# An attention and expert-routing kernel whose instruction order is searched anew

## The chip, the cores and the metric

The kernel runs on one core of a Trainium2 chip. The metric is the device time of one execution in microseconds (us). The kernel before takes 164.45 us, the median of three runs (163.86 to 164.68). One execution more was recorded by the hardware profiler, and everything that is read from a trace comes from that one.

The core's engines run their own instruction lists side by side. PE multiplies matrices into PSUM, DVE and ACT work on vectors, POOL does small work, and SP issues DMAs. An engine takes its instructions strictly in the order of its list and stands still until what the next one needs is there.

## The reference

The input x holds 4 batches of 11,456 rows of 128 numbers; there are 32 inducing rows, and 8 experts of two layers each. Two attentions follow each other, and the result goes through a layer of experts, of which each row takes the best one:

```python
def mab(q, kv):
    s = scale * (q @ kv.transpose(0, 2, 1))
    s = s - s.max(-1, keepdims=True)
    a = np.exp(s)
    a /= a.sum(-1, keepdims=True) + 1e-09
    return a @ kv
h = mab(I, x)
return mab(x, h).astype(np.float32)
...
logits = x @ w_gate
expert_idx = np.argmax(logits, axis=1)
...
    h = np.maximum(xe @ w1[e], 0.0)
    ye = h @ w2[e]
    out[mask] = gate_w[mask, None] * ye
```

The first attention sums over all rows of a batch, so the second can begin only when the batch's 32 rows of h are complete. What the experts see is a mixture of 32 rows, so the kernel applies the batch's expert to these 32 rows once and mixes the results.

## The kernel before

Each batch is cut into 6 groups; group g of batch b has the number k = 6b + g, from 0 to 23. A group is one load of xT (960 KB, tile `big`), and 19 such tiles hold loaded xT, a second form xn of it, and output on its way out. Ten groups load xn as well. For the 14 others PE turns the loaded xT (15 blocks of 128x128) and ACT or DVE copy the result out of PSUM.

For a group the first attention takes a score product (`scores`, 4 matmuls in the list, which the trace records as 8), the maximum, the exponential on ACT, a transpose on DVE, and an H sum (`h_sum`, 15 matmuls in the list, 30 in the trace). After the sixth group a short sequence on DVE, POOL and PE makes the batch's h, its centred form `hc`, the expert's result `h4`, and fetches the expert's weights (1024 KB, `fetch`, issued by ACT into the only `wt` tile).

The second attention reads the same xT tile again: a score product with `hc`, the exponential, and, four groups at a time, a logits product, then gate weights on DVE, a spread product (`spread`), a multiplication on DVE, four expert products (`experts`), four copies to an output tile by ACT or DVE (`evict`), and a store (960 KB). The tile of xT is free once the score product with `hc` has read it. The tile of xn is free once its H sum has read it.

What runs when is set by a program ahead of the chip. `make_plan` writes all operations with what they depend on, `schedule` sorts them into one list per engine, and the kernel is that list. `schedule` plays the execution through with assumed durations and picks, for each engine that is free, the ready operation with the lowest rank. The ranks come from the table `PLAN`. `schedule` also gives out the tiles, so what a load has to wait for follows from the order. In the played execution SP holds back a load or a store while `INFLIGHT` of them are under way:

```python
            if busy[e] > t or (e == "SP" and inflight >= INFLIGHT):
                continue
```

The finished kernel has no such rule. SP waits only for the semaphores that say that the tile is free.

Of the kernel before, what the change touches and what calls it, by code (L numbers as in the profile page):

```python
# [18 lines left out]
B, N, C, M, E, F = 4, 11456, 128, 32, 8, 1024  # L19
P = 128  # L20
# [14 lines left out]
HOP, SAME, FREE, RATE, PAUSE, AGAIN, FIRST = 70, 35, 40, 420, 400, 1200, 490000  # L35
SWITCH, STICK, INFLIGHT, BEHIND = 145, 10990, 2, 27149
# [23 lines left out]
class Lines:  # L60
# [3 lines left out]
    def put(self, o, when):  # L64
        queue, size, weight, start, _ = o.dma
        q, when = self.queues.setdefault(queue, []), when + start
        if queue == "SP" and not q and when - self.last > PAUSE:
            when += AGAIN
        q.append([when, size, weight, o, queue == "SP"])
# [41 lines left out]
def schedule(ops, caps, groups):  # L111
# [54 lines left out]
    while done < len(ops):  # L166
# [75 lines left out]
BYTES = 983040  # L242
LAG = 1060

PLAN = {
    "A": [
        17166, 30860, 22659, 17269, 6624, 4373, 4782, 13983, 33870, 18093, 7605, -6153, 10338, 6743, 1815, -6765,
        12145, 1215, 9171, -11099, 2829, -22378, 9660, 7139,
    ],
    "L": [  # L250
        -22577, -20358, -30968, -27201, -21639, -28610, -16795, -17141, 1480, -31968, -33025, 11502, -3904, 4335,
        11351, 18051, 6540, 8404, 16971, 4643, 15711, 27260, 33194, 28410,
    ],
    "N": [
        7261, 4545, -2957, -33356, 1585, 22336, 20181, -13380, -8654, 15944, 12613, -23335, -3583, -3966, -18329,
        -12841, 6354, 12743, 12327, -31853, 14534, 13707, 30755, 17389,
    ],
    "S": [
        -18320, 7796, 9352, -1925, -14397, -7386, -4476, 18662, 2319, 11122, 3399, -23370, -43944, -18219, -21050,
        -10585, 11208, -34837, 40042, 5734, 21165, 11776, 34515, -3269,  # L260
    ],
    "R": [
        -44906, 56, -24232, -58472, -48981, -57542, -36224, -33903,
    ],
    "X": [
        -31666, 10454, -45613, -16798, -24345, -17218, -24300, 252, -42184, -7384, -58546, -46281, -23642, -37678,
        -7849, -31311, -64290, -24020, -13825, 3252, -15541, -22251, 1326, 1966,
    ],
    "C": [
        4873, -17403, -60296, -10236,  # L270
    ],
    "off": {
# [7 lines left out]
    },  # L280
    "own": {
# [155 lines left out]
def make_plan(K, plan):  # L437
# [28 lines left out]
    for b in range(B):  # L466
        acc = nb_prev = None
        s1, m1, e1 = {}, {}, {}
        xn = {}
        for g in range(NG):  # L470
            k = b * NG + g
# [890 lines left out]
```

## Time and profile before

| quantity | value |
|---|---|
| median of three runs | 164.45 us (163.86 to 164.68) |
| the profiled execution | 164.66 us |
| its span, first to last instruction | 162.9 us |
| PE busy | 144.8 us, 89% |
| DVE busy | 123.0 us, 75% |
| ACT busy | 96.3 us, 59% |
| moved by DMA | 61.88 MB, mean 380 GB/s |

The span is what the trace shows; 1.76 us of the profiled execution's time lie around it. A busy share is a mean over stages with different limits, so the rows below are by stretch. [...] "To landing" is the time from the issue of a DMA to the moment at which its data has arrived; a DMA that waits behind others in the queue has that wait in it.

### The profile page before, as it was taken

How to read it: one execution, taken by the hardware profiler on the slowest of the kernel's cores; microseconds unless marked ns; L12 is line 12 of the kernel's file. 1: busy time of each engine (PE TensorE's matmuls, PEld its weight loads, DVE VectorE, ACT ScalarE, POOL GpSimd, SP SyncE). 2: the span in 40 equal slices, each digit the busy share in tenths (PEclk: the TensorE clock that was granted, in tenths of full speed). 3: DMA queues.
4: the chain of work that ended last, by engine and by line, in shares of the span. 5: the costliest groups of instructions: out<-in, count | busy, mean ns of one | idle time of the engine just before them, and what ended most of it. 6: DMA issues, size and time to landing. Idle time of an engine off the chain costs nothing.

```text
span 162.9 us, 5024 instructions
## 1 busy us (share of the span) xinstructions
PE 144.8 (89%) x1994; PEld 86.7 (53%) x1995; DVE 123.0 (75%) x350; ACT 96.3 (59%) x200; POOL 14.9 (9%) x78
## 2 busy tenths in 40 slices
PE   7799999999989869999999999999999999997000
PEld 4096847789823635385756674565633455363000
DVE  0048569777569986999999999989999999896000
ACT  3043683564247358452687678698989888957000
POOL 0100000000000300021100001331050201120000
PEclk9999999999999999999999999999999999999555
DMA  5999999999999999999998998989999999999991
GB/s 162 428 428 428 419 428 430 417 405 344 365 399 336 426 416 429 394 424 427 423 383 295 260 396 334 415 303 364 423 373 292 427 426 424 424 424 422 416 410 51
DMA packets 9102, 61.88 MB, mean 380 GB/s; under 512 B 1008, under 2 KB 1136, under 8 KB 8560
## 3 DMA queue, kind: packets, MB, share of 16 engines
q1 hardware_dynamic: 8352, 57.10, 87.4%
q10 hardware_dynamic: 720, 4.39, 7.3%
q8 instruction: 17, 0.28, 0.7%
q14 instruction: 13, 0.11, 0.2%
HBM read 37.89 MB, written 23.59 MB: 377 GB/s over the span
## 4 chain that ended last, share of the span: by engine, by line
PE 76%; DMA 12%; DVE 2%; ACT 1%; issue 1%; SPq 0%; DVEq 0%
PE bank L717 21%; PE bank L1019 17%; PE bank L728 14%; PE bank L770 10%; DMA big<-in_xT 9%; PE bank L1012 5%; DMA csb<-in_consts 3%; PE bank L681 3%; PE bank L956 3%; ACT big L736 1%; PE bank L879 1%; PE bank L857 1%; DVE mx L720 0%; DVE mid L961 0%; DVE mid L760 0%
## 5 line engine op out<-in xcount | busy, mean ns | idle before, releaser
L736 ACT COPY big<-bank 128x480 f32<-128x480 f32 (+2 forms) x124 | 61.4, 588 | 31.3 <-PE bank L728 23.2
L1019 PE MATMUL bank<-mid,h 32*128 32x480 f32 x192 | 34.1, 602 | 0.4 <-ACT big L736 0.4
L728 PEld LDWEIGHTS bank<-csb,big 128*128 128x128 f32 x210 | 23.8, 145 | 7.0 <-issue 3.5
L728 PE MATMUL bank<-csb,big 128*128 128x128 f32 x210 | 26.1, 282 | 1.3 <-DVE rs L983 1.3
L717 PE MATMUL bank<-big,csb 128*32 128x480 f32 x192 | 24.5, 589 | 2.3 <-DMA big<-in_xT 1.2
L720 DVE TENSOR_REDUCE mx<-bank 128x1 f32<-128x480 f32 x24 | 15.4, 648 | 11.2 <-PE bank L717 10.4
L770 PE MATMUL bank<-big,mid 128*32 128x129 f32 x720 | 23.8, 274 | 0.0
L770 PEld LDWEIGHTS bank<-big,mid 128*32 128x32 f32 x720 | 21.2, 110 | 4.3 <-issue 3.0
L952 ACT ACTIVATE mid<-bank,nb 128x480 f32<-128x480 f32 x24 | 15.4, 663 | 13.1 <-DVE nb L947 11.2
L1019 PEld LDWEIGHTS bank<-mid,h 32*128 32x128 f32 x192 | 17.0, 183 | 10.3 <-ACT big L736 3.7
L738 DVE COPY big<-bank 128x512 f32<-128x512 f32 (+2 forms) x28 | 17.5, 650 | 5.9 <-PE bank L728 5.2
L717 PE MATMUL bank<-big,hc 128*32 128x480 f32 x192 | 21.4, 568 | 0.0
L757 ACT ACTIVATE mid<-bank,mx 128x480 f32<-128x480 f32 x24 | 14.9, 664 | 3.6 <-DVE mx L754 3.6
L760 DVE STREAM_TRANSPOSE mid<-mid 128x480 f32<-128x480 f32 x24 | 15.2, 652 | 0.7 <-ACT mid L757 0.7
L943 DVE TENSOR_REDUCE mx<-bank 128x1 f32<-128x480 f32 x24 | 14.9, 631 | 1.0 <-PE bank L717 0.9
L1012 PE MATMUL bank<-mid,sel 32*128 32x480 f32 x48 | 15.1, 603 | 0.0
L1015 DVE TENSOR_TENSOR mid<-mid,bank 128x480 f32<-128x480 f32 x24 | 14.8, 644 | 0.2
L717 PEld LDWEIGHTS bank<-big,csb 128*32 128x32 f32 x192 | 5.5, 111 | 9.4 <-issue 3.6
L717 PEld LDWEIGHTS bank<-big,hc 128*32 128x32 f32 x192 | 5.4, 111 | 9.2 <-issue 5.1
L1012 PEld LDWEIGHTS bank<-mid,sel 32*128 32x128 f32 x48 | 5.3, 183 | 3.0 <-ACT big L736 1.4
L956 PE MATMUL bank<-mid,gzb 128*32 128x480 f32 x48 | 6.2, 572 | 0.0
L939 POOL COPY thr_all<-thr 32x1 f32<-32x1 f32 x24 | 4.3, 180 | 9.8 <-DVE thr L932 8.9
(96 smaller groups left out, 117.3 us busy)
## 6 DMA issues: line engine op xcount, KB each, us to landing
big<-in_xT SPq DMA_DIRECT2D x24, 960.0 KB, 10.4
out<-big SPq DMA_DIRECT2D x24, 960.0 KB, 6.8
big<-in_xn SPq DMA_DIRECT2D x10, 967.5 KB, 8.7
wt<-in_w ACTq DMA_DIRECT2D x4, 1024.0 KB, 10.4
csb<-in_consts ACTq DMA_DIRECT2D x1, 194.5 KB, 5.5
```

The source lines that it names most:

```text
L717: self.nc.tensor.matmul(self.blk(ps[32 * q : 32 * q + 32, :GW]), lhsT=lhsT, rhs=x[:, :, q, :], start=True, stop=True)
L720: self.nc.vector.tensor_reduce(self.mx1[b][g // 2][:, g % 2 : g % 2 + 1], self.bank(fe)[:, :GW], AX.X, ALU.max)
L728: self.nc.tensor.transpose(ps[:, k * P : (k + 1) * P], x[:, k0 + k].rearrange("p q t -> p (q t)"), self.ident)
L736: self.nc.scalar.copy(dst, src)
L738: self.nc.vector.tensor_copy(dst, src)
L757: self.nc.scalar.activation(self.at(e), self.bank(fe)[:, :GW], AF.Exp, bias=self.mx1[b][p + 1][:, 2:3], scale=SCALE)
L760: self.nc.vector.transpose(self.at(e), self.at(e))
L770: self.nc.tensor.matmul(ps[32 * j : 32 * j + 32, : P + 1], lhsT=e[:, k, :], rhs=x[:, k, :], start=(n < 4), stop=(n >= 2 * GB - 4))
L943: self.nc.vector.tensor_reduce(self.mx2[r][:, u : u + 1], self.bank(fe)[:, :GW], AX.X, ALU.max)
L952: self.nc.scalar.activation(self.at(e), self.bank(fe)[:, :GW], AF.Exp, bias=self.nb2[r][:, u : u + 1])
L1012: self.nc.tensor.matmul(self.bank(s)[:, :GW], lhsT=self.sel[rows], rhs=self.at(lv)[rows], start=True, stop=True)
L1019: self.nc.tensor.matmul(self.bank(o)[:, :GW], lhsT=self.h4[b][rows], rhs=self.at(e)[rows], start=True, stop=True)
```

## The change

The operations and their number are the same. The search that found the table `PLAN` was run again with another picture of the queue in `schedule`: SP may have three DMAs under way instead of two, so two may be queued behind the one in progress, and a load's data is assumed to start 3000 ns after its issue instead of 1000 (`LEAD`), except at the start of the kernel. Two other constants of the sorting changed, and nearly every number of `PLAN`, of which the diff shows the ranks of the xT loads. `PLAN` also says which engine makes some of the copies out of PSUM: DVE now makes 32 of the copies to `big` tiles instead of 28, ACT 120 instead of 124.

```diff
@@ -33,7 +33,7 @@
 
 
 HOP, SAME, FREE, RATE, PAUSE, AGAIN, FIRST = 70, 35, 40, 420, 400, 1200, 490000
-SWITCH, STICK, INFLIGHT, BEHIND = 145, 10990, 2, 27149
+SWITCH, STICK, INFLIGHT, BEHIND = 145, 10693, 3, 17877
 COLD, IDLE, WINDOW = 6500, 3000, 3400
 ENGINES = ("PE", "DVE", "ACT", "POOL", "SP")
 
@@ -63,8 +63,9 @@
 
     def put(self, o, when):
         queue, size, weight, start, _ = o.dma
+        start = min(start, 1000) if when < 1500 else start
         q, when = self.queues.setdefault(queue, []), when + start
-        if queue == "SP" and not q and when - self.last > PAUSE:
+        if queue == "SP" and not q and when - self.last > PAUSE and start < 2000:
             when += AGAIN
         q.append([when, size, weight, o, queue == "SP"])
 
@@ -241,186 +242,187 @@
 GROUPS = {"mid": (18, {"e1": 6, "e2": 13, "lv": 4}), "bank": (8, {"fe": 6, "o": 8, "mi": 3, "sp": 3}), "big": (19, {"xt": 17, "xn": 6, "ob": 6})}
 BYTES = 983040
 LAG = 1060
+LEAD = 3000
 
 PLAN = {
...
     "L": [
-        -22577, -20358, -30968, -27201, -21639, -28610, -16795, -17141, 1480, -31968, -33025, 11502, -3904, 4335,
-        11351, 18051, 6540, 8404, 16971, 4643, 15711, 27260, 33194, 28410,
+        -33798, -16984, -29552, -24749, -21692, -32969, -33305, -29006, -15841, -4369, 7132, -20776, 12552, 5655,
+        11228, 16108, 6631, 5749, 16403, 5868, 14901, 28644, 33347, 29138,
     ],
...
@@ -472,7 +474,7 @@
             xt = xts[k] = Buf("xt")
             xn[g] = Buf("xn")
             fe = Buf("fe")
-            ld = op(f"LT{k}", ("L", k, ""), {"SP": (400, 400)}, lambda xt=xt, b=b, g=g: K.load_xt(xt, b, g), take=[xt], dma=("SP", BYTES, 7680, 1000, LAG))
+            ld = op(f"LT{k}", ("L", k, ""), {"SP": (400, 400)}, lambda xt=xt, b=b, g=g: K.load_xt(xt, b, g), take=[xt], dma=("SP", BYTES, 7680, LEAD, LAG))
             s1[g] = op(f"S1.{k}", ("A", k, "S1"), pe(800), lambda fe=fe, xt=xt: K.scores(fe, K.it_s, xt), [ld, warm], take=[fe], use=[xt], kind="C")
             m1[g] = op(f"M1.{k}", ("A", k, "M1"), {"DVE": dve(480)}, lambda fe=fe, b=b, g=g: K.max1(fe, b, g), [s1[g]], use=[fe])
             if g in TURNED[b]:
@@ -484,7 +486,7 @@
                     tr = op(f"TR{k}.{n}", ("A", k, "TR"), pe(110 * m), lambda o=o, xt=xt, k0=k0, m=m: K.turn(o, xt, k0, m), [ld, on], take=[o], use=[xt], kind="F")
                     xr.append(op(f"TE{k}.{n}", ("A", k, "TE"), {"ACT": act(m * 128), "DVE": dve(m * 128)}, lambda e, o=o, xn=xn[g], k0=k0, m=m: K.turn_out(e, o, xn, k0, m), [tr, on], use=[o, xn[g]]))
             else:
-                xr = [op(f"LN{k}", ("N", k, ""), {"SP": (400, 400)}, lambda xn=xn[g], b=b, g=g: K.load_xn(xn, b, g), take=[xn[g]], dma=("SP", 990720, 7740, 1000, LAG))]
+                xr = [op(f"LN{k}", ("N", k, ""), {"SP": (400, 400)}, lambda xn=xn[g], b=b, g=g: K.load_xn(xn, b, g), take=[xn[g]], dma=("SP", 990720, 7740, LEAD, LAG))]
             e1[g] = (fe, Buf("e1"), xr)
             if g % 2:
                 p = g // 2

```

In the lists a tile has its buffer number behind its name, so the same number stands again when the buffer is used again. The line numbers of the new kernel are two higher.

The first place is SP, the loads that follow the first eleven. `in_xT` and `in_xn` are the two forms of a group. In the list of before this was:

```order
L708 DMA big_103<-in_xn 128x1935
L705 DMA big_94<-in_xT 128x1920
L708 DMA big_88<-in_xn 128x1935
L708 DMA big_90<-in_xn 128x1935
L705 DMA big_103<-in_xT 128x1920
L705 DMA big_92<-in_xT 128x1920
L708 DMA big_88<-in_xn 128x1935
L708 DMA big_90<-in_xn 128x1935
L705 DMA big_101<-in_xT 128x1920
```

The fifth of these, into `big_92`, is batch 1, group 5. In the new list the loads from the twelfth on read:

```order
L707 DMA big_103<-in_xT 128x1920
L710 DMA big_91<-in_xn 128x1935
L710 DMA big_89<-in_xn 128x1935
L707 DMA big_99<-in_xT 128x1920
L710 DMA big_97<-in_xn 128x1935
L707 DMA big_102<-in_xT 128x1920
L707 DMA big_91<-in_xT 128x1920
L710 DMA big_93<-in_xn 128x1935
L710 DMA big_97<-in_xn 128x1935
L707 DMA big_90<-in_xT 128x1920
```

Batch 1, group 5 is now the first of the rows (`big_103`), ahead of every load that waits for a tile; the xn load into `big_91` and another into `big_89` follow it. The last row, `big_90`, is batch 2, group 3.

The second place is PE, at the first score product of batch 3, group 0 (in `big_97` before, in `big_98` now) and the transposes of batch 2, group 4 (L728 before, L730 now; in `big_93` before, in `big_94` now). Before, it read:

```order
L717 MATMUL bank_83<-big_101,csb 32x480 x4
L681 MATMUL bank_79<-mq_0_151,csb 32x8 x4
L681 MATMUL bank_78<-csb,hacc_170 32x32 x4
L681 MATMUL bank_78<-csb,hacc_170 32x128 x4
L717 MATMUL bank_82<-big_97,csb 32x480 x4
L956 MATMUL bank_81<-mid_117,gzb_195 32x480
L956 MATMUL bank_81<-mid_121,gzb_195 32x480
L956 MATMUL bank_81<-mid_120,gzb_195 32x480
L956 MATMUL bank_81<-mid_115,gzb_195 32x480
L728 MATMUL bank_84<-csb,big_97 128x128 x4
L728 MATMUL bank_77<-csb,big_97 128x128 x4
L728 MATMUL bank_78<-csb,big_93 128x128 x4
```

Now it reads:

```order
L958 MATMUL bank_77<-mid_104,gzb_195 32x480
L719 MATMUL bank_82<-big_98,csb 32x480 x4
L719 MATMUL bank_78<-big_90,csb 32x480 x4
L859 MATMUL bank_81<-wt_128,hT_all 32x256 x4
L730 MATMUL bank_79<-csb,big_98 128x128 x4
L730 MATMUL bank_77<-csb,big_90 128x128 x3
L730 MATMUL bank_84<-csb,big_93 128x128 x3
L730 MATMUL bank_83<-csb,big_93 128x128 x4
L730 MATMUL bank_81<-csb,big_93 128x128 x4
L730 MATMUL bank_79<-csb,big_90 128x128 x4
L730 MATMUL bank_77<-csb,big_94 128x128 x4
```

The score product of batch 3, group 0 now stands behind the four logits matmuls (L956 before, L958 now, of which the last is shown) instead of ahead of them, and eight other products and transposes stand between it and the first transpose of `big_94`, the last row.

The third place is SP again, where the loads end and the stores begin. Before:

```order
L708 DMA big_98<-in_xn 128x1935
L708 DMA big_100<-in_xn 128x1935
L708 DMA big_92<-in_xn 128x1935
L708 DMA big_99<-in_xn 128x1935
L711 DMA out<-big_90 128x1920
L711 DMA out<-big_102 128x1920
```

Now:

```order
L710 DMA big_103<-in_xn 128x1935
L710 DMA big_100<-in_xn 128x1935
L713 DMA out<-big_97 128x1920
L710 DMA big_96<-in_xn 128x1935
L710 DMA big_95<-in_xn 128x1935
L713 DMA out<-big_85 128x1920
L713 DMA out<-big_97 128x1920
```

The first store, batch 0, group 3 from `big_97`, now stands ahead of the last two xn loads (batch 3, groups 3 and 4, into `big_96` and `big_95`).

## Rows read from the trace of the kernel before

**Rows 1.** The page, its span and the DMA rate in 40 slices of 4.07 us.

```profile
span 162.9 us, 5024 instructions
...
GB/s 162 428 428 428 419 428 430 417 405 344 365 399 336 426 416 429 394 424 427 423 383 295 260 396 334 415 303 364 423 373 292 427 426 424 424 424 422 416 410 51
```

**Rows 2.** Windows: stretch, us, busy us of each engine (instructions), PEclk, DMA share, GB/s.

```profile
35.00:63.00 28.00, 25.43 (x449) 16.99 (x443) 21.40 (x64) 14.14 (x29) 1.50 (x8) 1.00 0.98 386
63.00:110.00 47.00, 47.00 (x820) 28.18 (x812) 44.87 (x135) 32.59 (x71) 5.76 (x24) 1.00 0.95 371
110.00:150.00 40.00, 39.45 (x342) 19.14 (x337) 37.61 (x105) 33.68 (x74) 6.45 (x29) 1.00 1.00 401
150.00:159.00 9.00, 0.00 (x0) 0.00 (x0) 0.31 (x1) 0.46 (x1) 0.00 (x0) 0.51 0.99 408
```

**Rows 3.** Windows of two short stretches among the stores.

```profile
109.20:110.40 1.20, 1.20 (x13) 1.01 (x11) 1.17 (x4) 1.20 (x4) 0.08 (x1) 1.00 0.29 116
121.00:126.00 5.00, 5.00 (x61) 1.63 (x53) 4.97 (x16) 4.10 (x9) 0.40 (x1) 1.00 1.00 288
```

**Rows 4.** Timeline of SP: start, length, queue, line, operation, tiles, count.

```profile
49.58 0.48 SPq L705 DMA_DIRECT2D big<-in_xT  x1
...
109.61 0.33 SPq L711 DMA_DIRECT2D out<-big  x1
...
150.91 1.22 SPq L711 DMA_DIRECT2D out<-big  x1
```

**Rows 5.** Single DMA issues at 31.1, 49.6, 85.5, 87.4, 109.6, 119.4, 150.9; all weights.

```profile
big<-in_xn SPq DMA_DIRECT2D x1, 967.5 KB, 6.5
...
big<-in_xT SPq DMA_DIRECT2D x1, 960.0 KB, 11.0
...
big<-in_xn SPq DMA_DIRECT2D x1, 967.5 KB, 5.2
...
big<-in_xn SPq DMA_DIRECT2D x1, 967.5 KB, 7.6
...
out<-big SPq DMA_DIRECT2D x1, 960.0 KB, 5.2
...
out<-big SPq DMA_DIRECT2D x1, 960.0 KB, 11.1
...
out<-big SPq DMA_DIRECT2D x1, 960.0 KB, 10.5
...
wt<-in_w ACTq DMA_DIRECT2D x4, 1024.0 KB, 10.4
```

**Rows 6.** Chain of waits from 36 to 62 us: start, length, what.

```profile
39.66 7.19 DMA big<-in_xT
...
48.77 7.58 DMA big<-in_xT
```

**Rows 7.** Timeline of PE from 44 to 62 us, in brackets its idle time before.

```profile
46.90 1.01 PE L717 MATMUL bank<-big,csb 128*32 128x480 f32 x8 [0.62 <-DMA big<-in_xT]
...
56.49 1.01 PE L717 MATMUL bank<-big,csb 128*32 128x480 f32 x8 [0.62 <-DMA big<-in_xT]
...
60.67 1.50 PE L728 MATMUL bank<-csb,big 128*128 128x128 f32 x12 [1.34 <-DVE rs L983]
```

**Rows 8.** Chain of waits from 62 to 112 us, pieces of PE work.

```profile
63.01 4.85 PE bank L717 x48
...
79.49 2.12 PE bank L728 x18
...
85.31 1.02 PE bank L1019 x8
...
95.76 1.64 PE bank L770 x58
...
97.72 1.82 PE bank L1019 x16
```

**Rows 9.** Groups of instructions on the page, copies by DVE out of PSUM.

```profile
L738 DVE COPY big<-bank 128x512 f32<-128x512 f32 (+2 forms) x28 | 17.5, 650 | 5.9 <-PE bank L728 5.2
```

More of the change, by code (lines that the diff above doesn't have):

```diff
@@ L243 @@
 LAG = 1060
+LEAD = 3000
 PLAN = {
     "A": [
-        17166, 30860, 22659, 17269, 6624, 4373, 4782, 13983, 33870, 18093, 7605, -6153, 10338, 6743, 1815, -6765,
-        12145, 1215, 9171, -11099, 2829, -22378, 9660, 7139,
+        23019, 16465, 14605, 4016, 8235, -5006, 18698, 8209, 31931, 5156, 28740, 8484, 15774, 5376, 2485, -6994, 9726,
+        564, 12848, -12061, 7232, -21889, 2871, 6032,
     ],
     "L": [
-        -22577, -20358, -30968, -27201, -21639, -28610, -16795, -17141, 1480, -31968, -33025, 11502, -3904, 4335,
@@ L252 @@
-        11351, 18051, 6540, 8404, 16971, 4643, 15711, 27260, 33194, 28410,
+        -33798, -16984, -29552, -24749, -21692, -32969, -33305, -29006, -15841, -4369, 7132, -20776, 12552, 5655,
+        11228, 16108, 6631, 5749, 16403, 5868, 14901, 28644, 33347, 29138,
     ],
     "N": [
-        7261, 4545, -2957, -33356, 1585, 22336, 20181, -13380, -8654, 15944, 12613, -23335, -3583, -3966, -18329,
-        -12841, 6354, 12743, 12327, -31853, 14534, 13707, 30755, 17389,
+        14859, -3991, -35877, -9960, 15490, 23016, 6301, 5869, 2417, 12463, 5576, -14356, -20784, -3863, -15512,
@@ L257 @@
+        12913, -25040, 10127, -3699, -32219, 14164, 14265, 31210, 22810,
     ],
     "S": [
-        -18320, 7796, 9352, -1925, -14397, -7386, -4476, 18662, 2319, 11122, 3399, -23370, -43944, -18219, -21050,
-        -10585, 11208, -34837, 40042, 5734, 21165, 11776, 34515, -3269,
+        -3135, 8839, -5624, 18962, 5944, 12481, 2599, -2133, -13438, -45084, -5120, -26084, -19766, -12050, 9815,
+        -22936, 11879, 39528, -35163, 20689, 9600, -17846, 3766, 34852,
     ],
     "R": [
-        -44906, 56, -24232, -58472, -48981, -57542, -36224, -33903,
+        -60685, 411, -23692, -35667, -60282, -52532, -48466, -39603,
@@ L264 @@
     ],
     "X": [
-        -31666, 10454, -45613, -16798, -24345, -17218, -24300, 252, -42184, -7384, -58546, -46281, -23642, -37678,
-        -7849, -31311, -64290, -24020, -13825, 3252, -15541, -22251, 1326, 1966,
+        -32728, -24789, -44871, -24463, -16335, -23899, -17517, -6557, -41985, -66, -60525, -49428, -35052, -24356,
+        -8704, -64107, -25092, 2831, 4527, -17532, -13122, 11444, -37303, 2055,
     ],
     "C": [
-        4873, -17403, -60296, -10236,
+        5735, -17544, -60623, -10971,
@@ L271 @@
     ],
     "off": {
[7 rows of a table removed]
[7 rows of a table added]
     },
     "own": {
[131 rows of a table removed]
[131 rows of a table added]
     },
     "ACT": [
[4 rows of a table removed]
[4 rows of a table added]
     ],
     "DVE": [
-        "PC0", "TE0.2", "TE10.0", "TE12.0", "TE13.1", "TE13.2", "TE16.0", "TE2.0", "TE2.3", "TE6.0", "TE6.3", "TE7.0",
-        "TE7.1", "TE7.3", "TE8.0", "TE8.2", "TE9.3", "V13.1", "V17.3", "V18.2", "V18.3", "V20.0", "V21.2", "V22.0",
-        "V22.2", "V22.3", "V23.0", "V4.0", "V9.2",
[3 rows of a table added]
     ],
```

287 rows, old and new, of the table PLAN are left out of this document.

## The prediction

> **What bounds the kernel now.** I read the slices first: the DMA rate lies near 428 GB/s in most of them [rows 1]. Then the stretches, which tell what is short where. From 63 to 110 us PE is busy for 47.00 us of 47.00, and from 110 to 150 for 39.45 of 40: there an order can win next to nothing on PE. From 35 to 63 it has 25.43 of 28, and these 2.6 us are what it can win. From 150 to 159 no engine computes to speak of and the DMA engines still move 408 GB/s [rows 2]: the end is a queue of stores that drains.
>
> So the end hangs on the last moment at which that queue was empty. This is 109.2 to 110.4 us, where the rate is 116 GB/s [rows 3], just when the sixth store (batch 1, group 4) is issued at 109.61 [rows 4]. It lands 5.2 us later, at 114.8. The last store, issued at 150.91 [rows 4], needs 10.5 us, to 161.4, because it waits in the queue [rows 5]. Between the two landings lie 46.6 us. A store of 960 KB at 428 GB/s takes 2.30 us; 18 of them are 41.4, the last weight load of 1024 KB is 2.4 [rows 5], and the remaining 2.8 are slow stretches such as 121 to 126 us at 288 GB/s [rows 3]. Moving that sixth store by a microsecond therefore moves the end by a microsecond, as long as no later store becomes the late one.
>
> What sets the sixth store is PE, which runs without a gap from 63 us to it. Before that it stood still three times, for 0.62, 0.62 and 1.34 us, together 2.6 [rows 7]. The chain names the causes. The score product at 46.90 waited for the load of batch 1, group 5, issued at 39.66 and 7.19 us under way. The one at 56.49 waited for the load of batch 3, group 0, issued at 48.77, 7.58 us under way [rows 6]. The wait before the transposes at 60.67 is put down to a DVE reciprocal [rows 7]; but those transposes read the load of batch 2, group 4, issued at 49.58 [rows 4], which took 11.0 us [rows 5] and so landed at the same 60.6. I count all three as late loads.
>
> **The change part by part.** The new constants and the LEAD line act only in the program that sorts the work: none is an instruction, and nothing on the chip limits the loads to two or three. SP issues a load as soon as its list reaches it and its tile is free. What can change the time is the lists. The pieces are the same: 24 loads of xT, 10 of xn, 24 stores, 291 pieces on PE.
>
> First, the late loads. Batch 1, group 5 moves from 17th load to 12th, and the first 12 wait for no tile; the full queue at the start delivers one load per 2.30 us, so it lands by about 33 us. The two others keep their kind of place, but the PE work between the product that frees their tile and the one that needs them grows. I use 0.81 us for a score product (4.85/6) and as much for a logits product, 0.85 for an H sum (1.64 for 58 of its 60 records in two), 0.12 per transposed block (2.12/18) [rows 8]. For batch 3, group 0 the work between was 6 score products, 2 H sums and small ones, 7.2 us, and the load needed 7.6; now it is 9 score products, 3 H sums and a logits product, 11.2. For batch 2, group 4 it was 9.0, and the load needed 11.0; now it is 13.9 (10 score products, 2 H sums, a logits product, 22 blocks, small ones). So these stalls go: minus 2.6.
>
> Second, what is late next. Loads that met a nearly empty queue needed 6.5 and 7.2 us, and at the end of the load phase 5.2 and 7.6 [rows 5, 6]. In the new list the load of batch 2, group 3 waits for the first score product with hc of batch 0, so the queue runs dry there; three more loads and the first weight load follow. Batch 2, group 4 is the third of them: 5.2 to 7.2 us, plus three times 2.30, plus up to 2.4 for the weights, is 14.5 to 16.5 us from that score product, and PE has 16.4 us of work before it needs it. That is 1.9 spare to 0.1 late. The score product of batch 2, group 0 comes about 7.0 us of work after the H sum that frees its load's tile, against 6.5 to 7.2 for the load. The first dozen loads are each needed within 1 us of their landing. I take 0.5 us for all of these together, between 0 and 1.5.
>
> [...]
>
> Third, PE's work ahead of the sixth store. In the order of before 183 pieces end with its last expert product; in the new one 185. The sets differ by two spread products and one expert product more, and one small product less, which I leave as nothing: 3 times 0.23 (1.82/8 [rows 8]) is 0.7. The new order changes its kind of product 32 times up to there, against 26: three more runs in and out. Two groups of experts in one run take 1.82 us and one alone 1.02 [rows 8], so a run costs 0.2; with the small product given back I take 0.3 for three. Together plus 1.0. The lower bound is 0.4 (the small product as dear as a piece, no price for the runs), the upper 1.5.
>
> Fourth, evictions. DVE takes four more copies from PSUM to the big tiles (32 against 28), ACT four fewer; 4 times 0.65 us is 2.6 [rows 9]. DVE has only 2.1 us free from 63 to 110 and 2.4 from 110 to 150 [rows 2]. At most one more than before lies ahead of the sixth store. The others fall into the tail, where the last store waits 10.5 less 5.2, that is 5.3 us, in the queue: this cover hides them, so I cost them at 0; without it they would cost up to 2.6. The 12th store has 1.3 us more PE work ahead of it than its counterpart; the 11th took 11.1 us to land [rows 5], so there the queue covers some 5.9.
>
> The sum: minus 2.6, plus 0.5, plus 1.0 is minus 1.1. The profiled execution took 164.66 us, 162.9 of span [rows 1] and 1.76 around it; the median of the three runs is 164.45, 0.2 less. I take the sum from the median: 163.3. With the bounds of its terms (minus 2.2 to minus 0.1, and 1.2 more if half of DVE's copies are not covered) the forecast's own range is 162.2 to 164.4, at worst 165.6.
>
> **The rivals.** *The stalls move.* Every early load lands close to its need, and the load phase stays paced at 2.30 us a load. If the products of batch 2, groups 0 and 4, stall for 1.5 us, minus 2.6 plus 1.5 plus 1.0 leaves 164.4. For it speak the three such stalls of before; against it, that PE now has 11 and 14 us where it had 7 and 9.
>
> *A store in front of two loads.* In before all 34 loads precede the first store. Now the store of batch 0, group 3 stands ahead of the xn loads of batch 3, groups 3 and 4, and SP issues them only after that store's four evictions. Between the H sum that frees the first tile and the H sum that needs it lie 7.3 us of PE work. Of the last two xn loads of before, one took 5.2 us and one 7.6, when a store was queued right behind it [rows 5]. If both now take 2 us longer than the dearer one, because the store's data goes first, they land 9.6 us after that H sum: PE, in order, stands still for 2.3 us near 95 us and the sixth store is late by it. That gives 163.3 plus 2.3, or 165.6, and it decides from 7.3 us of landing time on.
>
> *The tail loses less.* The weight load among the stores goes with 288 GB/s from 121 to 126 us, 1.6 us lost [rows 3]. It still stands behind the same product, so I expect it again; if the loss goes, the time is 161.7.
>
> That the list changes nothing can be excluded: PE's order differs almost everywhere.
>
> **How the numbers follow.** Forecast 0.50, moving stalls 0.25, the store ahead of loads 0.15, the lighter tail 0.10. A measurement of this kernel tells about 0.5% (0.8 us) from no change. So faster is below 163.6: 0.36 of the forecast's half, the tenth of the lighter tail and 0.05 of the moving stalls, 0.51. Slower is above 165.3: 0.11 of the store rival, 0.03 of moving stalls that cost more, 0.02 of uncovered copies, 0.16. Within 0.5% lies the rest, 0.33. The range for 8 in 10 goes from 161.4, a little below the lighter tail, to 165.4, just short of the store rival.
>
> **What would show it.** Right: no wait of PE for an xT load between 35 and 63 us, and PE busy there for nearly 28 of 28; the sixth store issued near 108.5; the DMA rate full from there on; the last store still waiting 4 us or more in its queue. Wrong: PE idle on loads at the score product of batch 2, group 0 or the transposes of group 4 (the first rival); PE idle on xn loads near 92 to 97 us (the second); or a last store that lands 5 us after its issue, which would mean that DVE or ACT had become the end.

## The result and the profile after

The new order is slower. It takes 166.35 us, the median of 11 executions (164.94 to 167.90); the kernel before took 164.32 in 11 beside it (163.40 to 165.73). The ratio is 1.0115, with a 95% interval of 1.0080 to 1.0149. A second and a third series gave 1.0139 [1.0074, 1.0203] and 1.0143 [1.0096, 1.0190]. Forecast were 163.3 us and a range of 161.4 to 165.4. Throughout, a ratio leaves out executions more than 1.5% above the fastest of their kernel, and a median is over all; in series that spread widely the two can differ, and both are then given.

The profiled execution took 165.75 us, 164.0 of it span. Its page, span and slices of 4.10 us, and the copies by DVE:

```profile
span 164.0 us, 5024 instructions
...
GB/s 149 426 423 429 418 420 420 425 426 369 313 414 268 368 427 418 425 423 419 419 417 370 404 212 384 195 377 419 433 412 432 420 431 416 425 425 427 427 246 19
...
L740 DVE COPY big<-bank 128x480 f32<-128x480 f32 (+2 forms) x32 | 20.1, 650 | 3.2 <-PE bank L730 3.0
```

The stretches of [rows 2] and [rows 3], in the same columns (PEclk is PE's granted clock, 1.00 at full speed):

```profile
35.00:63.00 28.00, 27.23 (x550) 17.70 (x546) 22.52 (x67) 12.55 (x25) 2.33 (x10) 1.00 0.95 368
63.00:110.00 47.00, 46.68 (x759) 27.23 (x753) 44.86 (x135) 34.30 (x73) 3.93 (x18) 1.00 0.93 370
110.00:150.00 40.00, 37.05 (x336) 18.41 (x328) 38.10 (x103) 31.52 (x67) 6.52 (x29) 1.00 1.01 423
150.00:159.00 9.00, 0.40 (x6) 0.30 (x2) 1.25 (x7) 0.62 (x2) 1.07 (x6) 0.70 0.93 384
...
104.00:105.70 1.70, 1.70 (x24) 0.54 (x19) 1.70 (x6) 0.71 (x2) 0.07 (x1) 1.00 0.62 76
121.00:126.00 5.00, 5.00 (x60) 1.90 (x52) 5.00 (x15) 2.99 (x8) 0.70 (x3) 1.00 1.00 418
```

From 35 to 63 us PE won 1.8 us. From 110 to 150 it lost 2.4, and now it, DVE and POOL still compute after 150. The store queue runs dry near 104 to 107 us (76 GB/s up to 105.7, then 126), not at 109.2; from 107 us on it is nearly full, also where the weight load had cost 1.6 us. The sixth and the last store, in SP's timeline ([rows 4]) and in the list of DMA issues (KB, us to landing; [rows 5]):

```profile
108.79 0.33 SPq L713 DMA_DIRECT2D out<-big  x1
...
150.69 1.20 SPq L713 DMA_DIRECT2D out<-big  x1
```

```profile
out<-big SPq DMA_DIRECT2D x1, 960.0 KB, 6.3
...
out<-big SPq DMA_DIRECT2D x1, 960.0 KB, 11.8
```

Both are issued earlier than before (109.61 and 150.91), and yet the last one lands at 162.5 instead of 161.4. What is new at the end is in the chain of waits (start, length, what), in all rows but the first, which is used further down:

```profile
142.09 1.67 DVE big L740 x3
...
150.48 0.17 DVE thr L934
150.69 0.08 issue
150.77 0.18 POOL thr_all L941
...
152.69 0.40 PE bank L1032 x2
153.11 0.16 DVE nleft L1033
```

The rows from 150.48 on are the threshold of batch 3 and, behind it, `count_left`: how many rows are not surely routed. Its result `nleft` is what every engine reads at the end to decide whether it runs the general part or jumps over its code (`tc.If(nl > 0)`, L1138, L1136 before). In the old list this chain stood ahead of the last expert products; in the new one it is the last entry of all. In the old list DF3, the threshold's matmul on PE, started at 142.6 us, and now it does at 149.6. The branch, by line: queue, instruction, count, ns, first and last start. First the kernel before, then the one after:

```profile
L1136 SPq EVENT_SEMAPHORE  x9: 17/17/17, 152.7 to 161.5; - x9
...
L1136 PEldq EVENT_SEMAPHORE  x2: 51/51/51, 155.9 to 156.1; - x2
...
L1136 PEldq COMPARE_BRANCH  x1: 6702/6702/6702, 149.2 to 149.2; - x1
```

```profile
L1138 SPq EVENT_SEMAPHORE  x9: 17/17/17, 154.9 to 162.6; - x9
...
L1138 PEldq EVENT_SEMAPHORE  x2: 51/51/51, 161.6 to 161.8; - x2
...
L1138 PEldq COMPARE_BRANCH  x1: 7385/7385/7385, 154.2 to 154.2; - x1
```

SP's last semaphore here is the landing of the last store. PE sits 6.7 and 7.4 us in its branch. Before, it is out 5.4 us ahead of the last landing; now 0.8 us ahead. So in this profile the last landing still sets the end.

Why does the last store land later, though it left earlier? A store lands in 16 parts, and the trace has the time of each. Fifteen of them are down at 160.3 us, 0.9 earlier than before (161.2); the last one comes at 162.5, 2.2 us behind them, where before it came 0.3 behind. A gap of this size (1.6 to 3.1 us) stands in four of the twenty profiles, those whose PE branch begins between 153.9 and 154.7 us: this one, warm_tail, count_last and count_last2. In the other sixteen it is 0 to 1.0 us. The DMA rate in slices of 0.4 us from 150 us on shows the tail that it makes, first before, then after:

```profile
GB/s 384 480 403 384 480 403 422 462 367 424 405 365 403 403 481 365 384 499 384 499 307 348 213 174 77 38 58 0 0 0 0 0 0 0 0 0 0 0 0 0
...
GB/s 403 461 365 422 499 403 422 403 422 480 403 403 442 403 461 403 403 480 403 269 219 38 38 0 38 19 19 38 40 19 41 0 0 0 0 0 20 0 0 0
```

Whether the packets of instructions, of which this profile has seven from 157 us on, hold this part up isn't shown: the trace does not tell which of the 16 DMA engines carries a packet.

In the third series the profile shows PE and the last landing the other way round:

```profile
L1138 SPq EVENT_SEMAPHORE  x9: 17/17/17, 158.0 to 161.4; - x9
...
L1138 PEldq EVENT_SEMAPHORE  x2: 51/51/51, 162.7 to 162.9; - x2
...
L1138 PEldq COMPARE_BRANCH  x1: 5358/5358/5358, 157.3 to 157.3; - x1
```

The stores are down at 161.4, no later than before, and the program waits for PE's branch until 162.9, since the count came 2.7 us later still: this branch begins at 157.3. Why, the windows of that profile say (columns as in [rows 2]):

```profile
142.00:144.00 2.00, 1.09 (x8) 0.34 (x8) 2.00 (x5) 0.60 (x2) 0.00 (x0) 1.00 1.01 419
144.00:146.00 2.00, 1.00 (x8) 0.61 (x10) 1.97 (x6) 0.00 (x0) 0.40 (x1) 0.57 1.01 422
146.00:148.00 2.00, 2.00 (x13) 1.13 (x8) 1.47 (x3) 1.03 (x3) 0.00 (x0) 0.50 1.03 430
148.00:150.00 2.00, 2.00 (x14) 1.76 (x12) 1.22 (x2) 0.45 (x1) 0.00 (x0) 0.50 0.89 373
150.00:152.00 2.00, 2.00 (x15) 0.92 (x8) 1.78 (x4) 1.51 (x4) 0.00 (x0) 0.73 0.82 334
```

Behind two waits of PE the granted clock is at 0.50, the lower of the two levels that the traces show (1.00 and 0.50), from about 145 to 151 us. Two such waits of 1.1 us stand in eight of the nine profiles of the new order without the filling matmuls below, also in those whose clock stays up, as in the first one (its PE waits from 110 us on: us in all, times, longest):

```profile
PE bank L1032 <- DVE cnt L1030: 2.7, 1, 2.7
PE bank L1021 <- DVE u L921: 1.1, 1, 1.1
PE bank L1014 <- DVE mid L1010: 1.1, 1, 1.1
PE bank L859 <- DMA wt<-in_w: 0.7, 1, 0.7
```

### The profile page after: what moved, and what is told of

It reads as the page before. It is cut to its first block, busy times and chain, and to the rows that moved or that the text cites. A ratio compares the mean times of both kernels' runs of the same rounds, so it can differ in the third digit from the quotient of the medians.

```text
span 164.0 us, 5024 instructions
## 1 busy us (share of the span) xinstructions
PE 144.0 (88%) x1994; PEld 85.2 (52%) x1995; DVE 125.2 (76%) x356; ACT 94.3 (58%) x194; POOL 14.9 (9%) x78
## 4 chain that ended last, share of the span: by engine, by line
PE 57%; DVE 23%; ACT 4%; issue 4%; DMA 3%; POOL 1%; DVEq 0%; POOLq 0%; ACTq 0%
PE bank L719 18%; PE bank L730 14%; PE bank L772 13%; PE bank L1021 5%; DVE mid L1017 4%; DVE mx L945 4%; DMA csb<-in_consts 3%; ACT big L738 3%; PE bank L683 2%; PE bank L1014 2%; DVE big L740 2%; PE bank L958 2%; DVE rs L985 1%; DVE nb L949 1%; DVE se L1004 1%
## 5 line engine op out<-in xcount | busy, mean ns | idle before, releaser
L738 ACT COPY big<-bank 128x480 f32<-128x480 f32 (+2 forms) x120 | 59.2, 594 | 27.5 <-PE bank L730 17.7
L730 PEld LDWEIGHTS bank<-csb,big 128*128 128x128 f32 x210 | 23.6, 145 | 8.3 <-issue 6.3
L730 PE MATMUL bank<-csb,big 128*128 128x128 f32 x210 | 26.2, 282 | 0.0
L772 PE MATMUL bank<-big,mid 128*32 128x129 f32 x720 | 24.5, 274 | 0.8 <-issue 0.8
L719 PE MATMUL bank<-big,csb 128*32 128x480 f32 x192 | 23.7, 587 | 1.2 <-DMA csb<-in_consts 1.2
L1021 PEld LDWEIGHTS bank<-mid,h 32*128 32x128 f32 x192 | 16.5, 183 | 12.5 <-issue 3.4
L740 DVE COPY big<-bank 128x480 f32<-128x480 f32 (+2 forms) x32 | 20.1, 650 | 3.2 <-PE bank L730 3.0
L1014 PE MATMUL bank<-mid,sel 32*128 32x480 f32 x48 | 12.6, 602 | 1.1 <-DVE mid L1010 1.1
L719 PEld LDWEIGHTS bank<-big,hc 128*32 128x32 f32 x192 | 6.1, 110 | 8.8 <-issue 5.9
L1014 PEld LDWEIGHTS bank<-mid,sel 32*128 32x128 f32 x48 | 4.1, 183 | 5.0 <-ACT big L738 3.8
L958 PE MATMUL bank<-mid,gzb 128*32 128x480 f32 x48 | 6.2, 571 | 0.0
```

The lines of the kernel that those rows point to most:

```text
L719: self.nc.tensor.matmul(self.blk(ps[32 * q : 32 * q + 32, :GW]), lhsT=lhsT, rhs=x[:, :, q, :], start=True, stop=True)
L730: self.nc.tensor.transpose(ps[:, k * P : (k + 1) * P], x[:, k0 + k].rearrange("p q t -> p (q t)"), self.ident)
L738: self.nc.scalar.copy(dst, src)
L740: self.nc.vector.tensor_copy(dst, src)
L772: self.nc.tensor.matmul(ps[32 * j : 32 * j + 32, : P + 1], lhsT=e[:, k, :], rhs=x[:, k, :], start=(n < 4), stop=(n >= 2 * GB - 4))
L1014: self.nc.tensor.matmul(self.bank(s)[:, :GW], lhsT=self.sel[rows], rhs=self.at(lv)[rows], start=True, stop=True)
```

## The experiments

Five theories stood against each other. A: the late count, by the branch behind it. B: the fifth store, which now meets the empty queue with a weight load ahead of it. C: one of the 16 DMA engines falls behind. D: PE's half clock in the tail. E: more work on PE costs its time. For each run stand the ratio to the kernel before on the same chip, and medians where they matter.

**The general part and the branch left out**, of the new and of the old order:

```diff
-    general_part(tc, K, xT, w, out)
```

> The changed kernel without the general part behind the branch (the part that corrects rows left over, none with this data) and without the branch itself; the count is still worked out. Theory A: the program ends with its last store, 2 to 3 us earlier, 163.3 to 164.4. Theories B and C: no change but for what a branch costs in any order, 165.8 to 166.4.

> The kernel before without the general part behind the branch and without the branch itself. Theory A: there the branch is decided early, and only what it adds behind the last store goes (the end of the program came 0.9 us after the last landing without it, 1.45 with it): 163.6 to 164.1. If a branch costs 1.6 us in any order, as it did in the changed kernel (166.35 to 164.78), 162.7 to 163.0.

Measured: 0.9982 [0.9942, 1.0022] (164.78 us) and 0.9917 [0.9876, 0.9957] (163.51). Both medians lie just outside A's ranges, by 0.4 us above and 0.1 below. The new order gains 1.3 to 1.6% by it, the old one 0.8%. So what hangs on the branch costs both, and the new order 0.5 to 0.8% more.

**The count left out, everything else in place**, first alone, then with three filling matmuls (below), beside the unchanged new order. DF3, th3, ts3 and LEFT are the threshold's matmul, its two steps on DVE and POOL, and the count:

```diff
+        nc.gpsimd.memset(self.nleft, 0)
...
+            if o.name in ("DF3", "th3", "ts3", "LEFT"):
+                continue
```

> The changed kernel without the threshold of batch 3 and without the count of rows left over; the branch stays and reads a zero written at the start (the count is zero for this data). Every store, and every instruction ahead of the last matmul, stands as in the changed kernel; only the decision comes about 3 us earlier, when the last copies are done. Theory A (late count): 0.8 to 1.6 us below the changed kernel on the same chip, ratio to the kernel before about 1.004. Theory D alone (half clock in the tail): no change to it, 1.012.

> The same with the three filling matmuls. Theories A and D together: both losses gone and no store later for it, ratio 0.993 to 1.001. A wrong: as warm_tail, 1.006. D wrong: as no_count.

> The changed kernel unchanged, as the other two's companion on the same chip: ratio 1.010 to 1.015. Theory D: its profile shows stretches at half clock between 130 and 150 us or, without them, a time in the lower half of its runs.

Measured: 0.9939 [0.9905, 0.9974], 0.9938 [0.9889, 0.9987], and 1.0143 [1.0096, 1.0190] for the unchanged order; medians 165.01, 164.58 and 166.90 (before: 164.30). So A holds, and is larger than expected: 1.9 us by the medians, of the 2.6 by which the unchanged order is slower beside it. Whether the rest is nothing or 0.7 us stays open, since the ratios put the two versions below the old order and the medians slightly above it. The branch rows of the first show why: PE is out of its branch 5.8 us ahead of the last landing.

```profile
L1142 SPq EVENT_SEMAPHORE  x9: 17/17/17, 153.6 to 161.6; - x9
...
L1142 PEldq EVENT_SEMAPHORE  x2: 51/51/51, 155.7 to 155.8; - x2
```

**The count moved**, three times. A small function takes the named operations out of the list and puts them behind another:

```diff
# count_first
+MOVES = (("dm3 dd3", "X19.1"), ("DF3", "SP20"), ("th3", "V18.3"), ("ts3", "th3"), ("LEFT", "X20.2"),)
# count_early
+MOVES = (("DF3", "X22.3"), ("th3", "W21"), ("ts3", "th3"), ("LEFT", "X21.1"),)
# early_both: count_early and, ahead of it in the table
+         ("V8.3", "W6"), ("V8.2", "V8.1"), ("OUT8", "V8.2"),
```

> The changed kernel (166.35 us, the kernel before 164.32) with the threshold chain of batch 3 and the count of rows left over (margin, diagonal, threshold, LEFT) taken from the very end of the order to where the kernel before has them, ahead of the last experts. Theory A (the late count: the branch at the end is decided at 153.3 us instead of about 149, and what the engines fetch then runs among the last stores and ends after them): 1.5 to 2.5 us less than the changed kernel, 163.9 to 164.9. Theory B (the queue of stores is last empty before the fifth store, with a weight load ahead of it, and all stores behind come late from there): no change, 166.2 to 166.5. Theory C (one of the 16 DMA engines falls behind the others, whatever the order): no change.

> The changed kernel with the diagonal's matmul, the threshold and the count of rows left over moved in among the last experts, each at a place where its input is already there (the first try, count_first, made the last stores wait, since it put VectorE's part in front of the last gate). The count should be there at about 150 instead of 153.2 us, and the last store be issued at about 152, behind a full queue. Theory A (late count): the program ends with its last store again, 1.5 to 2.5 us below the changed kernel: 163.9 to 164.9 where that has 166.35. Theories B and C: no change.

> As count_early, and the last two evictions of the fifth store put ahead of two others, so that it is issued at about 102.7 instead of 104.43 us and its data runs before the weight load, while the sixth store (108.8) stays where it is. Theory B: the sixth store is then the last that finds the queue empty, and all behind it lands 1.1 us earlier: 162.8 to 163.8. Theory A alone: as count_early, 163.9 to 164.9.

Measured: 1.0138 [1.0051, 1.0225], 1.0242 [1.0166, 1.0318] and 1.0130 [1.0075, 1.0185]. All three miss by A, up to 5 us (169.83 for the second). Their profiles led to D: the second has PE at half clock twice, from 134 to 137 and from 148 us on, and its last store leaves at 158.4 us instead of 150.7.

**The clock held up.** At three places where PE waits, a matmul that nothing reads:

```diff
+FILL = ("G3", "SP22", "X22.0")
+def fill(K, o):
+    if o.name in FILL:
+        K.nc.tensor.matmul(K.bank(o.take[0])[:, 0:384], lhsT=K.ones, rhs=K.ones.unsqueeze(1).to_broadcast([P, 3, P]), start=True, stop=True)
```

> The changed kernel with one matmul that nothing reads (0.85 us at full clock) ahead of each of three places in the tail where TensorE waits about 1.1 us (the third expert load's first product G3, the last spreads, the last experts). Theory D (in the tail TensorE waits, after such waits its clock is at half for about 3 us in a part of the executions, and the last stores and the count come up to 4 us later there): the granted clock stays 1.00 from 128 to 150 us, the slow executions go, and the median falls by 0.5 to 1.2 to 165.3 to 166.0, where the count at the end still holds it. Theory A (late count alone): no change, 166.3 to 166.8. Theory E (the added TensorE work lengthens its chain): up to 2.5 us more, 168.

> The same three matmuls, and the threshold and the count moved in among the last experts as in count_early. Theories A and D together: the program ends with its last store, which is issued at about 152 behind a full queue: 163.6 to 164.6. Theory A without D: as count_early, 168 to 170. Theory D without A: as warm_tail.

> As warm_count, and the fifth store's last two evictions put first, as in early_both. With D in place the last stores no longer find the queue empty, and theory B can show itself: 0.8 to 1.1 us below warm_count, 162.6 to 163.6; if the tail decides anyway, no change to warm_count.

> As warm_tail, without the general part behind the branch and the branch itself. Theories A and D together: the changed order then has neither loss, and stands against the kernel before without that part (163.51 us) as its stores do: 162.5 to 163.5. Theory A alone: 164.8 as without the three matmuls.

Measured: 1.0060 [1.0018, 1.0102] (166.30 us), 1.0104 [1.0065, 1.0143], 1.0074 [1.0038, 1.0111] and 0.9931 [0.9886, 0.9976]. Of the clock D is right, of two times not: warm_tail's median misses D's 165.3 to 166.0, and warm_no_rest's (164.13) the 162.5 to 163.5, though the old order beside them took 165.13 and not 164.32. In all seven profiles with the filling matmuls the granted clock is 1.00 from 128 to 152 us, as in this one (warm_tail):

```profile
128.00:150.00 22.00, 21.17 (x158) 9.54 (x154) 20.89 (x49) 15.72 (x34) 2.69 (x11) 1.00 1.01 424
```

Of the nine profiles of the new order without them five show stretches at half clock in the tail (the second and third series, count_first, count_early, no_rest); the second series in the same window:

```profile
128.00:150.00 22.00, 18.89 (x138) 8.75 (x138) 19.28 (x50) 14.65 (x32) 2.69 (x11) 0.92 0.96 395
```

E is out, as the added matmuls made nothing slower. count_early fell from 1.0242 to 1.0104 by them, with intervals apart. In the unchanged order the gain is 0.5 to 0.8%, and there the intervals overlap. There the last store left later in the profiles with half clock in the tail: 43.7 and 44.7 us behind the sixth in the second and third, 41.9 in the first. How much of this reaches the end isn't shown. The third profile, with some 6 us at half clock, spans 164.1 us, the first one without any 164.0, and the second 166.1, but there the sixth store already left 1.6 us later. Of the 11 executions of the first series the three with the lowest mean clock (0.940 to 0.953) took 166.58, 166.00 and 164.94 us, where the median is 166.35.

warm_count missed by A again, with the clock held: in its profile, the longest of its twelve executions (167.41), the first of its last three stores left at 153.95, in warm_tail's at 148.84. Of these 5.1 us 1.7 lie ahead of the sixth store, 1.5 are a longer wait for the last weight load, and the remaining 1.9 I put down to what the moved steps hold up on PE and DVE, which no run of its own shows. (A wait for POOL's copies, which the next expectation names, is not in its rows.)

**The count moved further ahead**, and the old order with its count at the end, in two series:

```diff
# warm_first (with FILL); warm_best has early_both's three moves besides
+MOVES = (("dm3 dd3", "X19.1"), ("DF3", "CT5"), ("th3", "V18.0"), ("ts3", "th3"), ("LEFT", "X20.2"),)
# count_last, count_last2 (on the kernel before)
+MOVES = (("DF3", "X20.3"), ("th3 ts3 LEFT", "OUT22"),)
```

> The changed kernel with the three filling matmuls, and the threshold taken ahead of the last spreads (its matmul lies in TensorE's wait there) and the count to the middle of the last experts, so that the copies on GpSimd are over when VectorE comes to the count (in warm_count VectorE stood in front of them, and the last three stores were issued 3 us later for it). Theories A and D together: count at about 149, last store issued by 151 behind a full queue; the program ends with its last store: ratio to the kernel before 0.996 to 1.002. Theory A wrong: as warm_tail, 1.006.

> As warm_first, and the fifth store's last two evictions put first, so that the weight load of batch 2 runs behind it. If the sixth store decides once the tail is mended (theory B): 0.8 to 1.1 us below warm_first, ratio 0.990 to 0.997. If the tail or the branch still decides: as warm_first.

> The kernel before (164.32 us) with its threshold chain of batch 3 and its count moved to the very end, behind the last eviction, as the changed kernel has them. Theory A: 1.5 to 2.5 us more, 165.8 to 166.8. Theories B and C: no change, 164.2 to 164.5, since the stores are issued as before.

> The same kernel as count_last (the kernel before with its threshold and count at the very end), since its first runs were spread over 5 us. Theory A: median of all runs 1.0 to 2.0 us above that of the kernel before. Otherwise within 0.4 of it.

Measured: 0.9984 [0.9939, 1.0028], 1.0014 [0.9962, 1.0065], 0.9993 [0.9941, 1.0046] and 0.9983 [0.9935, 1.0032]. The first lies inside what A and D together forecast (0.996 to 1.002), the second does not show the gain of B. With the count early and the clock held the new order is even with the old one; it isn't faster. The opposite move leaves A undecided. The ratios say no change; the medians lie 1.8 and 1.0 us up (166.44 on 164.63, 165.92 on 164.89), as A's two forecasts had them, the second at its lower edge. In the profile of count_last2 the count is as late as in the new order (the branch begins at 154.0). PE is out at 160.8, but the last store lands at 162.9, its last part 1.6 us behind the fifteenth; in the kernel before it landed at 161.5.

```profile
L1151 SPq EVENT_SEMAPHORE  x9: 17/17/17, 154.7 to 162.9; - x9
...
L1151 PEldq EVENT_SEMAPHORE  x2: 51/51/51, 160.7 to 160.8; - x2
```

**The fifth store alone**, its last eviction put behind hc2 (the centred h of batch 2, on DVE), two others held back, and the weight load behind the store:

```diff
+MOVES = (("V8.3", "hc2"), ("V0.0 V0.1", "V8.2"), ("OUT8", "V0.1"), ("GA2", "OUT8"),)
```

> The changed kernel with the evictions of the fifth store put ahead of others on VectorE and ScalarE, and the weight load of batch 2 behind that store: its issue at about 102.7 instead of 104.43 us. Theory B: the sixth store (108.79) becomes the last to find the queue empty; it lands at 114.0 instead of 115.1, all behind it 1.1 us earlier, 165.2. Theory A: the decision still falls at 153.3, and only a shorter queue in front of the fetches helps: 0 to 0.6 us less, 165.8 to 166.4. Theory C: no change.

Measured: 1.0167 [1.0105, 1.0229]. It moved the weight load to 107.0 us and with it the sixth store, to 110.86, so it says little. early_both, warm_both and warm_best made the cleaner move (fifth store 1.8 us nearer to the fourth, weight load behind it) and show no gain that their intervals could tell: B is not seen.

**The changed order again:**

> The changed kernel unchanged, beside the others on the same chip. Theory A: its profile has the branch of TensorE or VectorE ending within 1.5 us of the last store's landing or after it, and 166.0 to 166.7. Theory C: one of the 16 DMA engines is the last by 3 us or more again, from the third weight load on; without that, the time falls to 164.5.

Measured: 1.0139 [1.0074, 1.0203]. Its last store lands at 163.1, and PE leaves its branch at 164.9. The last part of that store comes 0.5 us behind the fifteenth, so C's lag is gone at the end, and the time did not fall: the loss does not need C. In the first profile, though, such a lag of 2.2 us is what made the last landing late.

## Why the prediction was wrong, point by point

- *The end is a queue of stores that drains.* This step failed. It was read off a stretch (150 to 159 us) in which the old order had nothing else left, and taken over to the new one. There the count comes last, and the branch behind it is left 1.8 and 1.5 us after the last landing in the second and third series. In the first profile the landing still comes last, by 0.8 us, but 2.2 us of it are one late part out of 16. No term of the sum had the count, and no rival. Leaving it out gives 1.9 us, of the 2.6 by which the new order was slower in the third series.
- *The signs of being right.* They came: no PE wait for xT from 35 to 63 us, the sixth store at 108.79, a full rate from there on, a last store that waits in its queue; only PE's 27.23 of 28 fell short. The time was longer all the same, since none of these signs looked at what stands behind the last store.
- *The forecast's own range.* Its bounds do not add up: minus 2.6, plus 1.5 and plus 1.5 is plus 0.4, not minus 0.1, so the range goes to 164.9, and at worst to 166.1. 166.35 lies above both.
- *The three load stalls go, minus 2.6.* Right: no wait for xT from 35 to 63 us in the first profile, 0.2 us in the third series. But 0.8 us came back as a wait of an H sum at 40.25, so PE won 1.8.
- *New late loads, plus 0.5.* No xT load was late in the first profile, so 0 would have been nearer. What was late was the weight load: 0.7 us of PE in the first profile, 1.7 in the third series.
- *More work ahead of the sixth store, plus 1.0.* In the first profile the store came 0.8 us earlier, near the forecast 1.1. In twelve profiles that share the new order up to there its issue lies between 107.81 and 110.39, mean 109.27; in four of the old order between 108.52 and 110.35, mean 109.56. So the gain is 0.3 with a spread of 2.6, and the 0.8 of the one pair was in good part luck.
- *DVE's four more copies are covered.* For the last store, yes (150.69). What I left out is that a busy DVE lets PE wait, 1.1 and 1.1 us near 142 and 144. Ahead of the second wait three copies by DVE stand in the chain of the first profile, from 142.09 us on; that these are among the four more was not tested. Behind such waits the clock fell to 0.50 in the third series, from about 145 us on, and not in the first profile. In the second series it fell earlier, to 0.50 between 133 and 137 us, behind a wait for the weight load. The fall cost time where the count is early (count_early: 1.0242, and 1.0104 with the clock held); in the unchanged order the last store left 1.8 and 2.8 us later behind the sixth where the clock fell, and what of that reaches the end isn't shown.
- *A microsecond at the sixth store is one at the end.* Not seen: it came 0.8 us earlier, the last landing 1.1 later. The other fifteen parts of the last store were down 0.9 earlier, which would fit, in one pair of profiles.
- *The rivals.* Moving stalls: no. A store ahead of two xn loads: no wait for xn. The lighter tail came true (418 GB/s from 121 to 126 us, 288 before), but the fifth store's low rate at 104 to 105.7 took its place.

What stays open: what the new order's stores are worth by themselves. Against the old order they give 0.9939 where only the count is gone. Where both lack the branch they give 0.9982 to 0.9917, and 0.9931 to 0.9917 with the filling matmuls, which is no gain. The count was not taken out of the old order, so what it costs there is not known. In the unchanged order the half clock's share of the loss is not shown.

## What to carry to other kernels

Before an end is put down to a draining queue, look up in the new order what each engine's list ends with, above all what a branch waits for; here a chain of small steps cost 1.9 us, by the medians, as the last entry. And look at PE's granted clock behind its waits where PE has become the path: in count_early it lay at 0.50 from 134 to 137 and from 148 us on, and the ratio was 1.0242, against 1.0104 with the clock held. No version here that computes the same beats the kernel before.

## What was not expected of the hardware

The branch takes 45 to 72 ns on POOL, DVE, ACT and SP, but PE stood in it for 5.4 us (third series) to 7.4 (first profile after), in nine profiles with a branch. From 150 us on no_count has 7 packets of instructions, the kernel before and the first and third series have 8 each, and the three profiles without the branch one each. In the 7 us from 157 us on, the first profile after has seven of them, 0.07 MB; the kernel before has three:

```profile
q1 hardware_dynamic: 80, 0.48, 17.8%
q8 instruction: 2, 0.03, 2.6%
q14 instruction: 5, 0.04, 1.5%
```

Whether PE's time in the branch has to do with these packets, no run shows.

Three filling matmuls, of 0.91 us each in the trace, in waits of about 1.1 us, went with a granted clock of 1.00 from 128 to 152 us in seven profiles of seven; without them it fell to 0.50 in the tail in five of nine.
